# Scores of two attention heads as 64-row products on the two row halves of the TensorE array

## The chip, the cores and the metric

The kernel runs on one core of a Trainium2 chip. The metric is device time in microseconds (us) for one execution. A profile is one further execution, taken by the hardware profiler; its engines are PE (TensorE matmul), PEld (TensorE weight load), DVE (VectorE), ACT (ScalarE), POOL (GpSimd) and SP (SyncE, which issues all loads and stores here).

## What is computed

A forgetting attention over 8 batches, 8 heads, 576 positions and 64 dimensions per head, and after it a channel mix on the 8 x 64 = 512 joined dimensions. All inputs are float32 or wider; shapes and the parts that matter:

```python
scores = scale * np.matmul(q, k.transpose(0, 1, 3, 2))
causal = np.triu(np.ones((S, S), dtype=bool), k=1)
cum = np.cumsum(np.maximum(s, 0.0), axis=-1)
bias = -(cum[:, :, :, None] - cum[:, :, None, :])
scores = np.where(causal, -1000000000.0, scores + np.minimum(bias, 0.0))
scores = scores - np.max(scores, axis=-1, keepdims=True)
attn = np.exp(scores)
attn = attn / (np.sum(attn, axis=-1, keepdims=True) + 1e-09)
x = np.matmul(attn, v)        # heads joined to 512 columns

xk = mu_k * x + (1.0 - mu_k) * x_prev      # x_prev: x one position earlier
xr = mu_r * x + (1.0 - mu_r) * x_prev
k = np.maximum(xk @ w_k, 0.0)              # 512 -> 1024
out = 1.0 / (1.0 + np.exp(-(xr @ w_r))) * (k * k @ w_v)
```

## The kernel before

**Precision.** Matmuls run on the type float32r, a rounded float32. To keep more bits, an operand is split into a high part (a rounded copy, made by ACT) and a low part (what is left, a subtraction on POOL or DVE), and a product is the sum of several matmuls over such parts in one bank of PSUM.

**Planner.** Nothing is issued in the order of the code. Each operation is added to a `Plan` (lines 54 to 282) with its engine, an estimate of its time, the buffers it reads and writes and a due time. `run` lays out all operations with a list scheduler, forward and backward eight times, keeps the order with the shortest estimate and then emits each engine's instructions in that order. A buffer of a tag with n copies waits for the user n turns before it. Due times only rank what is ready; they hold nothing back.

**Visits.** A visit is one pair of heads of one batch. Batch 0 is visited in two passes, first the tiles 0 to 2 of the queries (`A`), then tiles 3 and 4 (`Z`), four pairs each; the seven later batches have 28 visits with all five tiles (`ALL`). Query tile t covers 64 rows for t = 0 and 128 otherwise, and 64, 192, 320, 448 or 576 keys: the keys up to its last row. Each visit loads Q and K (line 588), K's and Q's parts are made (lines 603 to 618), V is loaded and split (552 to 563), and then, for each head: scores, exponents, normalization, transposes of the attention weights on PE (line 770), their split (797, 801 and others), and the product with V (line 903) into `xT`, which goes to DRAM. Each 256 positions that are complete make one chunk of the channel mix: 18 chunks, matmuls at lines 1040 (w_k), 1082 (w_r) and 1107 (w_v). They fill PE between the attention's steps, and they alone are left after the last visit.

**Q and K.** `load_turned` (573) loads each head's Q and K with their 64 dimensions twice, into partitions 0 to 63 and again into 64 to 127 of one tile: four transfers for Q and four for K per visit. `split_qk` (595) makes for each head `KH`, the rounded K on both halves, and `KL`, the rest on both halves; and `G`, whose lower half is rounded Q and whose upper half is the rest of Q (a cast of 128 partitions on ACT, a subtraction of 64 on POOL). So a 128-row product of G with KH gives (high Q + low Q) times high K, and one with KL the same times low K.

**Scores.** `scores` (625) handles one head. It loads the prefix sums of the gate into `cb`, broadcast over the partitions (line 630); POOL makes from it the causal `mask` (649). `products` (661) takes one bank of the two of tag `s`, puts two matmuls into it (line 678), G with KH and G with KL, and has DVE read it (line 693): a fused add of the bias, scale and running minimum that writes the tile `W` and the negated maximum `nm`. A tile of 576 keys is done in two pieces of 288, so a head with all tiles has six pieces: 64, 192, 320, 448, 288 and 288 keys. Where a piece holds the diagonal block, DVE reads it in two instructions. Then ACT takes the exponent (711) and POOL multiplies by the reciprocal sum (724).

**Buffers.** `cb`, `mask` and `s` have two copies, `raw` four, `G`, `KH` and `KL` three. The score tiles `W` exist in two sets, used by the heads in turn; in the passes `A`, which need only the small tiles, two further sets lie inside the largest tile of each (`early`, 376 to 382).

**Order of a visit.** Line 1248: for each of the two heads in turn, its scores are added, then the weighted sum of the head before (`finish`, 1222); the next visit's preparation comes after the first head's scores. Loads are added one visit ahead (1242 to 1244).

Of the kernel before, what the change touches and what calls it, by code (L numbers as in the profile page):

```python
# [12 lines left out]
F32R = mybir.dt.float32r  # L13
# [272 lines left out]
def forgetting_attention_then_channel_mix(  # L286
# [64 lines left out]
    def dma(emit, reads, writes, ns):  # L351
# [21 lines left out]
        for u in range(2)  # L373
    ]

    early = [w[:3] for w in weights]
    for w in weights:
        early.append([])
        for t in range(3):
            c = sum(KN[:t])  # L380
            early[-1].append(fixed(w[NQ - 1].ap[:, c : c + KN[t]]))
        w[NQ - 1].last = early[-1]

    for w in early:
        nc.gpsimd.memset(w[0].ap[64:P], 0.0)
# [187 lines left out]
    def load_turned(src, b, hp, a, e, tag, plain):  # L573

        if plain:
            x = sbuf([P, e - a], tag, 3)
            dma(
                lambda: nc.sync.dma_start(
                    x.get(), src[b, 2 * hp : 2 * hp + 2, :, a:e].rearrange("h d t -> (h d) t")
                ),  # L580
                [], [(x, 0), (x, 1)], 819 * (e - a) / S,
            )
            return [x]
        xs = [sbuf([P, e - a], "raw", 4) for _ in range(2)]
        for j in range(2):
            for r in range(2):
                dma(
                    lambda j=j, r=r: nc.sync.dma_start(
                        xs[j].get()[64 * r : 64 * r + 64], src[b, 2 * hp + j, :, a:e]
                    ),  # L590
                    [], [(xs[j], r)], 410 * (e - a) / S,
                )
        return xs

    def split_qk(qs, ks):

        nq, nk = qs[0].n, ks[0].n
        G = [sbuf([P, nq], "G", 3, F32R) for _ in range(2)]
        KH, KL = ([sbuf([P, nk], x, 3, F32R) for _ in range(2)] for x in ("KH", "KL"))
        for j in range(2):  # L600
            k, kh, kl = ks[j], KH[j], KL[j]
            act(
                lambda k=k, kh=kh: nc.scalar.copy(kh.get(), k.get()),  # L603
                [(k, 0), (k, 1)], [(kh, 0), (kh, 1)], nk, 150,
            )
            pool(
                lambda k=k, kh=kh, kl=kl: nc.gpsimd.tensor_tensor(  # L607
                    out=kl.get(), in0=k.get(), in1=f32(kh.get()), op=ALU.subtract
                ),
                [(k, 0), (k, 1), (kh, 0), (kh, 1)], [(kl, 0), (kl, 1)], nk, 114, 2.21,  # L610
            )
            q, g = qs[j], G[j]
            act(
                lambda q=q, g=g: nc.scalar.copy(g.get(), q.get()),
                [(q, 0), (q, 1)], [(g, 0), (g, 1)], nq, 150,
            )
            pool(
                lambda q=q, g=g: nc.gpsimd.tensor_tensor(  # L618
                    out=g.get()[64:P], in0=q.get()[64:P], in1=f32(g.get()[64:P]), op=ALU.subtract
                ),  # L620
                [(q, 1)], [(g, 1)], nq, 114, 2.21,
            )
        return G, KH, KL

    def scores(b, h, tiles, G, KH, KL):

        NK = KN[tiles[-1]]
        CB = sbuf([P, NK], "cb", 2) if not first else first.pop(0)
        (b == 0 and h < 2 and tiles == A) or dma(
            lambda: nc.sync.dma_start(  # L630
                CB.get(), cum_d.ap[b * H + h : b * H + h + 1, 0:NK].broadcast_to([P, NK])
            ),
            [cum_d], [CB], 819 * NK / S,
        )
        nm, sums, rinv = (sbuf([P, n], x, 2) for x, n in (("nm", 3 * NQ), ("sums", NQ), ("rinv", NQ)))
        if 0 in tiles:
            pool(lambda: nc.gpsimd.memset(sums.get()[:, 0:1], 1.0), [], [(sums, 0)], 1, 36)
        pt = early[h % 4] if tiles == A else weights[h % 2]


        M = sbuf([P, S], "mask", 2)

        def mask(m, k0, n):
# [16 lines left out]

        def products(t, m, i, k0, w, W):
            ps = bank(1, "s", 2)
            q0 = QS[t] - QS[tiles[0]]
            if KL is None:
                r = slice(64 * (h % 2), 64 * (h % 2) + 64)
                pe(
                    lambda: nc.tensor.matmul(
                        ps.get()[:m, :w],
                        G.get()[r, q0 : q0 + m],
                        KH.get()[r, k0 : k0 + w],  # L670
                        start=True,
                        stop=True,
                    ),
                    [(G, x) for x in range(2)] + [(KH, x) for x in range(2)], [ps], w, m, 4 / 2.4, 64,
                )
            for x, K in enumerate((KH, KL) if KL is not None else ()):
                pe(
                    lambda x=x, K=K: nc.tensor.matmul(  # L678
                        ps.get()[:m, :w],
                        G.get()[:, q0 : q0 + m],  # L680
                        K.get()[:, k0 : k0 + w],
                        start=x == 0,
                        stop=x == 1,
                    ),
                    [(G, x) for x in range(2)] + [(K, x) for x in range(2)], [ps], w, m,
                )

            for a, e in ((k0, min(k0 + w, QS[t])), (max(k0, QS[t]), k0 + w)):
                if a >= e:
                    continue  # L690
                bias = CB if a < QS[t] else M
                dve(
                    lambda a=a, e=e, bias=bias, i=i: nc.vector.tensor_tensor_reduce(  # L693
                        out=W.ap[:m, a:e],
                        in0=ps.get()[:m, a - k0 : e - k0],
                        in1=bias.get()[:m, a:e],
                        scale=-SCALE,
                        scalar=3.0e38 if i == 0 else nm.get()[:m, 3 * t + i - 1 : 3 * t + i],
                        op0=ALU.add,
                        op1=ALU.min,  # L700
                        accum_out=nm.get()[:m, 3 * t + i : 3 * t + i + 1],
                    ),
                    [ps, (bias, 0 if bias is CB else t > 0)] + ([(nm, (t, i - 1))] if i else []),
                    [(W, i), (nm, (t, i))], e - a,
                )
                i += 1
            return i

        def exponents(t, m, n, mi, W):
# [12 lines left out]
        def normalize(t, m, n, W):  # L722
# [15 lines left out]
        if 0 in tiles:  # L738
            mask(64, 0, 1)
        mask(P, QS[max(1, tiles[0])], len([t for t in tiles if t]))  # L740
        for t in tiles:
            m, n, W = QN[t], KN[t], pt[t]
            i = 0
            for k0, w in [(0, n)] if n <= 512 else [(0, n // 2), (n // 2, n // 2)]:
                i = products(t, m, i, k0, w, W)
            exponents(t, m, n, i - 1, W)
        pool(
            lambda: nc.gpsimd.tensor_scalar(
                out=rs(rinv), in0=rs(sums), scalar1=1.0e-9, scalar2=None, op0=ALU.add
            ),  # L750
            [(sums, t) for t in tiles], [rinv], len(tiles), 100,
        )
        dve(lambda: nc.vector.reciprocal(rs(rinv), rs(rinv)), [], [rinv], 8 * len(tiles))  # L753
        for t in tiles:
            normalize(t, QN[t], KN[t], pt[t])
        return pt
# [435 lines left out]
    def load(n):  # L1192
        b, hp, tiles = visits[n]
        q0, q1 = QS[tiles[0]], QS[tiles[-1]] + QN[tiles[-1]]
        loaded[n] = (
            load_turned(q, b, hp, q0, q1, "G", n < PLAINQ),
            load_turned(k, b, hp, 0, q1, "KH", n < PLAINQ),
        )

    def prepare(n):  # L1200
# [3 lines left out]
        QKs[n] = (qs * 2, ks * 2, [None] * 2) if n < PLAINQ else split_qk(qs, ks)  # L1204
        Vs[n] = vn if n < PLAIN else split_v(vn, vn.n // P)
# [12 lines left out]
    pend = None  # L1218
# [20 lines left out]
    for n, (b, hp, tiles) in enumerate(visits):  # L1239
# [8 lines left out]
        for j in range(2):  # L1248
            plan.due = due + j * step
            pt = scores(b, 2 * hp + j, tiles, *(x[j] for x in QKs[n]))  # L1250
            if pend is not None:
                finish(*pend)
            pend = (j, pt, Vs[n], xT, n, due + (j + WDUE) * step)
# [53 lines left out]
```

## Time and profile before

| | |
|---|---|
| runs shown | 919.32, 919.80, 922.17 us; median 919.8 |
| profiled execution | span 919.5 us, beside which the profile gives no other time; its mean granted TensorE clock 0.965 |
| instructions | 18649 |
| moved by DMA | 110.89 MB; HBM read 90.64 MB, written 19.04 MB |
| loads of Q and K | 240 of 144 KB, 32 of 80 KB, 16 of 64 KB |
| prefix sums (`cb`) | 64 loads of 288 KB, 6 of 160 KB |
| transposes (line 770) | 960 matmuls |
| scores (line 678) | 768 matmuls |

How to read its views. The page gives each engine's busy time, its share of the span and its count of instructions, and the clock that the throttle granted to TensorE in 40 slices of the span (tenths of full speed). The view by stretches gives the same busy times for any part of the span, or for one line of the code. The groups of instructions give line, engine, operation, the names of the tiles written and read, the shape and the count. The timeline lists instructions by their start. Matmuls are pipelined, so the recorded length of one overlaps the start of the next, and the ends are modelled; a PE that is busy all the time may still wait a little in it. A wait is put down to the instruction that released it.

### The profile page before, as it was taken

What the parts mean: (1) busy time and instruction counts of PE and PEld (TensorE: products, weight loads), DVE (VectorE), ACT (ScalarE), POOL (GpSimd) and SP (SyncE); (2) the same over time, 40 slices, a digit from 0 to 9 for tenths busy, and PEclk for the clock granted to TensorE, in tenths of its full rate; (3) what the DMA queues carried; (4) which work ended last, traced back from release to release, by engine and by line L of the source; (5) the groups of instructions that cost most, each with busy time, mean ns of one, the idle gap of its engine ahead of it and who ended that gap; (6) DMA issues with size and microseconds to landing.
All of it is one profiled execution on the core that took longest, in us unless ns stands there. A gap on an engine that the chain in (4) does not pass through costs nothing. (4 is left out here: it accounts for less than half of the span.)

```text
span 919.5 us, 18649 instructions
## 1 busy us (share of the span) xinstructions
PE 872.8 (95%) x5546; PEld 758.6 (83%) x5546; DVE 696.3 (76%) x2473; ACT 693.1 (75%) x1834; POOL 519.1 (56%) x884
## 2 busy tenths in 40 slices
PE   6877879999999999999999999999999999998998
PEld 4656858987988898988889898989898979887886
DVE  6897998987987788778878778777787887546431
ACT  5888888998997898788968787878787876445331
POOL 6999599898576566556665646565556461100000
PEclk7568989999999999999999999999999999999999
DMA  6798645645344343434353525252434230101100
GB/s 195 223 257 237 206 123 160 174 142 168 100 151 129 109 152 87 145 112 144 100 151 93 163 61 159 79 152 79 147 97 138 79 89 25 42 31 35 46 24 23
DMA packets 65045, 110.89 MB, mean 121 GB/s; under 512 B 10544, under 2 KB 26416, under 8 KB 64944
## 3 DMA queue, kind: packets, MB, share of 16 engines
q1 hardware_dynamic: 64944, 109.71, 40.2%
q8 instruction: 43, 0.70, 0.3%
q14 instruction: 58, 0.48, 0.2%
HBM read 90.64 MB, written 19.04 MB: 119 GB/s over the span
## 5 line engine op out<-in xcount | busy, mean ns | idle before, releaser
L1040 PE MATMUL m<-xh,w_k 128*128 128x256 f32 x1152 | 231.4, 287 | 4.4 <-DVE kl L1069 4.4
L711 ACT ACTIVATE W<-W,nm 64x64 f32<-64x64 f32 (+4 forms) x320 | 179.7, 562 | 41.3 <-DVE nm L693 36.7
L770 PE MATMUL t<-ident,W 128*128 128x128 f32 (+1 forms) x960 | 188.3, 284 | 16.6 <-DVE ph L844 4.8
L1107 PE MATMUL m<-w_v,kh 128*128 128x512 f32 x576 | 198.4, 403 | 0.0
L1040 PEld LDWEIGHTS m<-xh,w_k 128*128 128x128 f32 x1152 | 186.2, 190 | 6.2 <-DVE kl L1069 4.8
L724 POOL TENSOR_SCALAR W<-W,rinv 64x64 f32<-64x64 f32 (+4 forms) x320 | 165.2, 538 | 10.6 <-DVE rinv L753 6.1
L1040 PE MATMUL m<-xl,w_k 128*128 128x256 f32 x576 | 164.6, 286 | 0.0
L770 PEld LDWEIGHTS t<-ident,W 128*128 128x128 f32 (+1 forms) x960 | 114.3, 133 | 47.5 <-DVE pl L801 7.9
L607 POOL TENSOR_TENSOR KL<-raw,KH 128x576 fp32r<-128x576 f32 (+1 forms) x72 | 98.5, 1370 | 79.8 <-ACT KH L603 73.4
L678 PE MATMUL s<-KH,G 128*128 128x288 f32 (+4 forms) x384 | 125.3, 335 | 11.3 <-ACT KH L603 5.3
L801 DVE TENSOR_TENSOR pl<-t,ph 128x256 fp32r<-128x256 f32 (+3 forms) x264 | 122.2, 472 | 16.0 <-ACT ph L797 14.7
L1107 PEld LDWEIGHTS m<-w_v,kh 128*128 128x128 f32 x576 | 106.2, 189 | 18.2 <-DVE r L530 0.2
L678 PE MATMUL s<-KL,G 128*128 128x288 f32 (+4 forms) x384 | 118.5, 312 | 2.4 <-POOL KL L607 2.4
L797 ACT CAST ph<-t 128x256 fp32r<-128x256 f32 (+3 forms) x264 | 107.3, 414 | 13.0 <-PE t L770 11.5
L1107 PE MATMUL m<-w_v,kl 128*128 128x512 f32 x288 | 117.0, 406 | 0.0
L693 DVE CUSTOM_DVE_ANT_0 W<-s,cb 128x320 f32<-128x320 f32 (+3 forms) x256 | 94.9, 375 | 26.4 <-PE s L678 21.7
L903 PE MATMUL po<-ph,V 128*128 128x448 f32 (+4 forms) x344 | 109.6, 326 | 3.7 <-ACT ph L797 1.8
L1040 PEld LDWEIGHTS m<-xl,w_k 128*128 128x128 f32 x576 | 109.2, 190 | 0.9
L618 POOL TENSOR_TENSOR G<-raw,G 64x576 fp32r<-64x576 f32 (+2 forms) x72 | 93.6, 1300 | 27.4 <-issue 13.2
L988 DVE SCALAR_TENSOR_TENSOR xp<-x,mu,xp 128x256 f32<-128x256 f32 (+3 forms) x192 | 80.4, 419 | 37.2 <-ACT xp L979 33.9
L979 ACT ACTIVATE xp<-x,mu 128x256 f32<-128x256 f32 (+3 forms) x192 | 81.5, 424 | 29.3 <-DVE xl L1011 9.7
L1082 PE MATMUL m<-w_r,xh 128*128 128x512 f32 x288 | 101.9, 407 | 0.0
(97 smaller groups left out, 1751.7 us busy)
## 6 DMA issues: line engine op xcount, KB each, us to landing
raw<-in_k SPq DMA_DIRECT2D x128, 144.0 KB, 3.2
cb<-cum_d SPq DMA_DIRECT2D x64, 288.0 KB, 3.6
raw<-in_q SPq DMA_DIRECT2D x112, 144.0 KB, 3.3
vn<-in_v SPq DMA_DIRECT2D x32, 320.0 KB, 3.8
out<-g SPq DMA_DIRECT2D x36, 256.0 KB, 2.1
x_d<-xT SPq DMA_DIRECT2D x28, 288.5 KB, 2.3
x<-x_d SPq DMA_DIRECT2D x12, 514.0 KB, 4.0
w_k<-in_moe_w_k SPq DMA_DIRECT2D x8, 512.0 KB, 5.3
```

What stands on the lines that cost most here:

```text
L607: lambda k=k, kh=kh, kl=kl: nc.gpsimd.tensor_tensor(out=kl.get(), in0=k.get(), in1=f32(kh.get()), op=ALU.subtract),
L678: lambda x=x, K=K: nc.tensor.matmul(ps.get()[:m, :w], G.get()[:, q0 : q0 + m], K.get()[:, k0 : k0 + w], start=x == 0, stop=x == 1,),
L693: lambda a=a, e=e, bias=bias, i=i: nc.vector.tensor_tensor_reduce(out=W.ap[:m, a:e], in0=ps.get()[:m, a - k0 : e - k0], in1=bias.get()[:m, ...
L711: lambda: nc.scalar.activation(W.ap[:m, :n], W.ap[:m, :n], AF.Exp, bias=nm.get()[:m, 3 * t + mi : 3 * t + mi + 1], scale=-1.0, accum_out=s ...
L724: lambda: nc.gpsimd.tensor_scalar(out=W.ap[:m, :n], in0=W.ap[:m, :n], scalar1=rinv.get()[:m, t : t + 1], scalar2=1.0, op0=ALU.mult, op1=AL ...
L770: lambda: nc.tensor.transpose(ps.get()[0:m, place : place + P], pt[t].ap[:, k0 : k0 + m], ident.ap),
L797: act(lambda: nc.scalar.copy(strips(ph), src()), [ps], [(ph, k) for k in ks], n * m)
L801: lambda: nc.vector.tensor_tensor(out=strips(pl), in0=src(), in1=f32(strips(ph)), op=ALU.subtract),
L903: lambda: nc.tensor.matmul(po.get()[: P if both else 64, at + q0 - base : at + q0 - base + m], V.get()[:, kb, 2 * j : 2 * j + (2 if both e ...
L1040: lambda u=u, f=f, c=c, n=n, w=w, x=x: nc.tensor.matmul(ps.get()[:, u * CT : (u + 1) * CT], weight["k", c, f // 4].get()[:, w, f % 4 * P : ...
L1082: lambda c=c, n=n, x=x, w=w: nc.tensor.matmul(ps.get(), x.get()[:, c, ts], weight["r", c, 0].get()[:, w], start=c == 0 and n == 0, stop=c ...
L1107: lambda f=f, n=n, x=x, w=w: nc.tensor.matmul(ps.get(), x.get()[:, f, ts], weight["v", f, 0].get()[:, w], start=f == 0 and n == 0, stop=f ...
```

## The change

The two heads of a visit lie side by side: the even head's 64 dimensions on partitions 0 to 63, the odd head's on 64 to 127. `load_pair` loads Q of both with one transfer, and K with another. `split_pair` makes a high and a low part of each tile, `QH` and `QL`, `KH` and `KL`, each for both heads at once, in two copies each. `scores` handles both heads. A piece takes both banks of `s`, one for each head, and puts three matmuls into each: high Q with high K, low Q with high K, high Q with low K (the product of the two low parts, which the kernel before contains, is left out). Each reads 64 partitions, the even head's the lower half and the odd head's the upper; the two heads' matmuls alternate, and the six are emitted as one operation of the planner. The stationary operand always has 128 columns, in the first piece too. DVE then reads the two banks as before.

With it go: four full sets of `W` in place of two with the two inner ones; four copies of the small sums; the weighted sums of the previous visit's two heads are added after this visit's scores of both; the next visit's preparation after those. A constructor's argument sets a smaller scratch space for dynamic DMA. The argument lists of `exponents` and `normalize` change to fit.

```diff
@@ -370,18 +370,9 @@
 
     weights = [
         [fixed(const.tile([P, KN[t]], F32, name=f"W{t}_{u}")) for t in range(NQ)]
-        for u in range(2)
+        for u in range(4)
     ]
-
-    early = [w[:3] for w in weights]
     for w in weights:
-        early.append([])
-        for t in range(3):
-            c = sum(KN[:t])
-            early[-1].append(fixed(w[NQ - 1].ap[:, c : c + KN[t]]))
-        w[NQ - 1].last = early[-1]
-
-    for w in early:
         nc.gpsimd.memset(w[0].ap[64:P], 0.0)
 
 
@@ -570,77 +561,39 @@
-    def load_turned(src, b, hp, a, e, tag, plain):
...
-        xs = [sbuf([P, e - a], "raw", 4) for _ in range(2)]
-        for j in range(2):
-            for r in range(2):
...
-    def split_qk(qs, ks):
...
-    def scores(b, h, tiles, G, KH, KL):
+    def load_pair(src, b, hp, a, e):
+
+        x = sbuf([P, e - a], "raw", 4)
+        dma(
+            lambda: nc.sync.dma_start(
+                x.get(), src[b, 2 * hp : 2 * hp + 2, :, a:e].rearrange("h d t -> (h d) t")
+            ),
+            [], [x], 819 * (e - a) / S,
+        )
+        return x
+
+    def split_pair(x, tag):
+
+        n = x.n
+        hi, lo = (sbuf([P, n], tag + y, 2, F32R) for y in "HL")
+        act(lambda: nc.scalar.copy(hi.get(), x.get()), [x], [hi], n, 150)
+        pool(
+            lambda: nc.gpsimd.tensor_tensor(
+                out=lo.get(), in0=x.get(), in1=f32(hi.get()), op=ALU.subtract
+            ),
+            [x, hi], [lo], n, 114, 2.21,
+        )
+        return hi, lo
+
+    def scores(b, hp, tiles, Q, K):
+        heads = (2 * hp, 2 * hp + 1)
+        QH, QL = Q
+        KH, KL = K
+        CBs, Ms, pts, stats = [], [], [], []
+
+        def mask(CB, M, m, k0, n):
...
@@ -658,55 +611,75 @@
-        def products(t, m, i, k0, w, W):
-            ps = bank(1, "s", 2)
...
-            for x, K in enumerate((KH, KL) if KL is not None else ()):
...
+        for h in heads:
+            CB = sbuf([P, NK], "cb", 2) if not first else first.pop(0)
+            (b == 0 and h < 2 and tiles == A) or dma(
+                lambda CB=CB, h=h: nc.sync.dma_start(
+                    CB.get(), cum_d.ap[b * H + h : b * H + h + 1, 0:NK].broadcast_to([P, NK])
+                ),
+                [cum_d], [CB], 819 * NK / S,
+            )
+            st = [sbuf([P, n], x, 4) for x, n in (("nm", 3 * NQ), ("sums", NQ), ("rinv", NQ))]
+            if 0 in tiles:
+                pool(
+                    lambda x=st[1]: nc.gpsimd.memset(x.get()[:, 0:1], 1.0),
+                    [], [(st[1], 0)], 1, 36,
+                )
+            M = sbuf([P, S], "mask", 2)
+            if 0 in tiles:
+                mask(CB, M, 64, 0, 1)
+            mask(CB, M, P, QS[max(1, tiles[0])], len([t for t in tiles if t]))
+            CBs.append(CB)
+            Ms.append(M)
+            stats.append(st)
+            pts.append(weights[h % 4])
+
+        def products(t, m, i, k0, w):
+            pss = [bank(1, "s", 2) for _ in heads]
+
+            def emit():
+                for n, (G, K) in enumerate(((QH, KH), (QL, KH), (QH, KL))):
+                    for j in range(2):
+                        r = slice(64 * j, 64 * j + 64)
+                        nc.tensor.matmul(
+                            pss[j].get()[:, :w],
+                            G.get()[r, q0 : q0 + P],
+                            K.get()[r, k0 : k0 + w],
+                            start=n == 0,
+                            stop=n == 2,
+                        )
+
+            x = plan.add(
+                "PE", max(3 * w * 1.0625 / 2.4, 330.0), emit, [QH, QL, KH, KL], pss, land=0.83 * P + 1
+            )
+            plan.columns[x] = 3 * w
+
+            for j in range(2):
+                ps, CB, M, (nm, _, _), W = pss[j], CBs[j], Ms[j], stats[j], pts[j][t]
+                y = i
+                for a, e in ((k0, min(k0 + w, QS[t])), (max(k0, QS[t]), k0 + w)):
+                    if a >= e:
+                        continue
+                    bias = CB if a < QS[t] else M
+                    dve(
...
+                        [(W, y), (nm, (t, y))], e - a,
+                    )
+                    y += 1
+            return y
+
+        def exponents(t, m, n, mi, W, nm, sums):
@@ -735,25 +708,28 @@
...
         for t in tiles:
+            m, n = QN[t], KN[t]
             i = 0
             for k0, w in [(0, n)] if n <= 512 else [(0, n // 2), (n // 2, n // 2)]:
+                i = products(t, m, i, k0, w)
+            for j in range(2):
+                exponents(t, m, n, i - 1, pts[j][t], *stats[j][:2])
+        for j in range(2):
...
@@ -1192,17 +1168,14 @@
     def load(n):
         b, hp, tiles = visits[n]
         q0, q1 = QS[tiles[0]], QS[tiles[-1]] + QN[tiles[-1]]
-        loaded[n] = (
-            load_turned(q, b, hp, q0, q1, "G", n < PLAINQ),
-            load_turned(k, b, hp, 0, q1, "KH", n < PLAINQ),
-        )
+        loaded[n] = (load_pair(q, b, hp, q0, q1), load_pair(k, b, hp, 0, q1))
 
     def prepare(n):
         qs, ks = loaded.pop(n)
         b, hp, tiles = visits[n]
         vn = load_values(b, hp, -(-KN[tiles[-1]] // P), n < PLAIN)
-        QKs[n] = (qs * 2, ks * 2, [None] * 2) if n < PLAINQ else split_qk(qs, ks)
-        Vs[n] = vn if n < PLAIN else split_v(vn, vn.n // P)
+        QKs[n] = split_pair(qs, "Q"), split_pair(ks, "K")
+        Vs[n] = split_v(vn, vn.n // P)
 
     plan.due = -3000.0
     loaded = {}
@@ -1245,17 +1218,17 @@
         plan.due = due
         xT = sbuf([P, S + 1], "xT", 2)
         pool(lambda xT=xT: nc.gpsimd.memset(xT.get()[:, 0:1], 0.0), [], [(xT, 2)], 1, 36)
-        for j in range(2):
-            plan.due = due + j * step
-            pt = scores(b, 2 * hp + j, tiles, *(x[j] for x in QKs[n]))
-            if pend is not None:
-                finish(*pend)
-            pend = (j, pt, Vs[n], xT, n, due + (j + WDUE) * step)
-            if j == 0 and n + 1 < len(visits):
-                plan.due = due + SPLIT * step
-                prepare(n + 1)
+        plan.due = due
+        pts = scores(b, hp, tiles, *QKs[n])
+        for x in pend:
+            finish(*x)
+        pend = [(j, pts[j], Vs[n], xT, n, due + (j + WDUE) * step) for j in range(2)]
+        if n + 1 < len(visits):
+            plan.due = due + SPLIT * step
+            prepare(n + 1)
         if n == len(visits) - 1:
-            finish(*pend)
+            for x in pend:
+                finish(*x)
         while done_chunks < NCHUNK:
             end = (done_chunks + 1) * CT - 1
             if end % S >= there[end // S]:
@@ -1276,7 +1249,7 @@
     import concourse.bacc as bacc
     from concourse.bass_utils import run_bass_kernel_spmd
 
-    nc = bacc.Bacc("TRN2", target_bir_lowering=False, num_devices=1)
+    nc = bacc.Bacc("TRN2", target_bir_lowering=False, num_devices=1, dynamic_dma_scratch_size=1024)
     arrays, args = {}, []
     for name in _INS:
         a = inputs[name]
```

More of the change, by code (lines that the diff above doesn't have):

```diff
@@ L595, in split_qk @@
-    def split_qk(qs, ks):
-        nq, nk = qs[0].n, ks[0].n
-        G = [sbuf([P, nq], "G", 3, F32R) for _ in range(2)]
-        KH, KL = ([sbuf([P, nk], x, 3, F32R) for _ in range(2)] for x in ("KH", "KL"))
-        for j in range(2):
[L601 to L623, printed above, removed]
@@ L625, in scores @@
-    def scores(b, h, tiles, G, KH, KL):
-        NK = KN[tiles[-1]]
[L628 to L643, printed above, removed]
+    def load_pair(src, b, hp, a, e):
[7 more added lines that the diff above has]
+        return x
@@ L659, in mask @@
             )
-        def products(t, m, i, k0, w, W):
-            ps = bank(1, "s", 2)
-            q0 = QS[t] - QS[tiles[0]]
[L664 to L675, printed above, removed]
-            for x, K in enumerate((KH, KL) if KL is not None else ()):
[L677 to L707, printed above, removed]
@@ L709, in exponents @@
-        def exponents(t, m, n, mi, W):
+        for h in heads:
[20 more added lines that the diff above has]
+            pts.append(weights[h % 4])
@@ new lines, in products @@
+        def products(t, m, i, k0, w):
+            pss = [bank(1, "s", 2) for _ in heads]
+            q0 = QS[t] - QS[tiles[0]]
+            def emit():
[21 more added lines that the diff above has]
+                    dve(
+                        lambda a=a, e=e, bias=bias, y=y, ps=ps, nm=nm, W=W: nc.vector.tensor_tensor_reduce(
+                            out=W.ap[:m, a:e],
+                            in0=ps.get()[:m, a - k0 : e - k0],
+                            in1=bias.get()[:m, a:e],
+                            scale=-SCALE,
+                            scalar=3.0e38 if y == 0 else nm.get()[:m, 3 * t + y - 1 : 3 * t + y],
+                            op0=ALU.add,
+                            op1=ALU.min,
+                            accum_out=nm.get()[:m, 3 * t + y : 3 * t + y + 1],
+                        ),
+                        [ps, (bias, 0 if bias is CB else t > 0)] + ([(nm, (t, y - 1))] if y else []),
+                        [(W, y), (nm, (t, y))], e - a,
+                    )
+                    y += 1
+            return y
@@ L720, in exponents, with normalize @@
             )
-        def normalize(t, m, n, W):
+        def normalize(t, m, n, W, rinv):
             pool(
@@ L736, in rs @@
             return x.get()[:, tiles[0] : tiles[-1] + 1]
-        if 0 in tiles:
-            mask(64, 0, 1)
-        mask(P, QS[max(1, tiles[0])], len([t for t in tiles if t]))
         for t in tiles:
-            m, n, W = QN[t], KN[t], pt[t]
+            m, n = QN[t], KN[t]
             i = 0
             for k0, w in [(0, n)] if n <= 512 else [(0, n // 2), (n // 2, n // 2)]:
[L745 to L756, printed above, removed]
+                i = products(t, m, i, k0, w)
+            for j in range(2):
+                exponents(t, m, n, i - 1, pts[j][t], *stats[j][:2])
+        for j in range(2):
+            _, sums, rinv = stats[j]
+            pool(
+                lambda sums=sums, rinv=rinv: nc.gpsimd.tensor_scalar(
+                    out=rs(rinv), in0=rs(sums), scalar1=1.0e-9, scalar2=None, op0=ALU.add
+                ),
+                [(sums, t) for t in tiles], [rinv], len(tiles), 100,
+            )
+            dve(
+                lambda rinv=rinv: nc.vector.reciprocal(rs(rinv), rs(rinv)),
+                [], [rinv], 8 * len(tiles),
+            )
+            for t in tiles:
+                normalize(t, QN[t], KN[t], pts[j][t], rinv)
+        return pts
     def weighted(j, pt, V, xT, tiles, plain):
@@ L1217, in forgetting_attention_then_channel_mix @@
         load_weight("r", c, 0, moe_w_r, R0 + RS * c, c)
-    pend = None
+    pend = []
     done_chunks = 0
@@ L1247, in forgetting_attention_then_channel_mix @@
         pool(lambda xT=xT: nc.gpsimd.memset(xT.get()[:, 0:1], 0.0), [], [(xT, 2)], 1, 36)
-        for j in range(2):
-            plan.due = due + j * step
-            pt = scores(b, 2 * hp + j, tiles, *(x[j] for x in QKs[n]))
-            if pend is not None:
-                finish(*pend)
-            pend = (j, pt, Vs[n], xT, n, due + (j + WDUE) * step)
-            if j == 0 and n + 1 < len(visits):
-                plan.due = due + SPLIT * step
-                prepare(n + 1)
+        plan.due = due
[6 more added lines that the diff above has]
+            prepare(n + 1)
         if n == len(visits) - 1:
-            finish(*pend)
+            for x in pend:
+                finish(*x)
         while done_chunks < NCHUNK:
```

16 lines of the change are left out of this document (removed).

## The prediction

> **What bounds the kernel now.** The page first: its span, the engines' busy shares, and the row of the granted TensorE clock in 40 slices.
>
> ```profile
> span 919.5 us, 18649 instructions
> PE 872.8 (95%) x5546; PEld 758.6 (83%) x5546; DVE 696.3 (76%) x2473; ACT 693.1 (75%) x1834; POOL 519.1 (56%) x884
> PEclk7568989999999999999999999999999999999999
> ```
>
> The profiled execution spans 919.5 us and the median of the runs shown is 919.8, so a sum made against the span needs no correction. PE is busy 95%, but an average over stages decides nothing, so next comes the busy time in three stretches (columns: length, busy time and instructions of PE, PEld, DVE, ACT and POOL, clock, DMA share, GB/s).
>
> ```profile
> 0.00:140.00 140.00, 108.02 (x556) 83.75 (x556) 120.66 (x408) 111.23 (x294) 117.13 (x205) 0.77 0.70 204
> 140.00:780.00 640.00, 631.86 (x4216) 560.08 (x4216) 514.19 (x1947) 527.86 (x1431) 399.15 (x674) 1.00 0.41 121
> 780.00:920.00 140.00, 132.88 (x777) 114.79 (x775) 61.44 (x120) 54.05 (x111) 2.80 (x6) 1.00 0.10 34
> ```
>
> From 140 to 780 us PE idles 8 of 640 us at a clock of 1.00: this stretch is as long as PE's instruction stream. The first 140 us are a ramp with four engines loaded (DVE 121, POOL 117, ACT 111 us) and PE idle for 32 us at a clock of 0.77. The last 140 us hold no scores. The list of waits agrees: what a score's load waits for its bank's reader is 13 us in all.
>
> ```profile
> PEld s L678 <- DVE nm L693: 13.0, 28, 1.2
> ```
>
> So a step off PE is worth time in the ramp at most, and a step on PE is worth its whole length in the 640 us, as far as the others keep up.
>
> **The change on PE.** A matmul's recorded length is modelled and overlaps the next, so I price by distance from start to start. The timeline (start, length, what):
>
> ```profile
> 501.48 0.19 PE L678 MATMUL s<-KH,G 128*64 128x64 f32 x1
> 501.51 0.22 PE L678 MATMUL s<-KL,G 128*64 128x64 f32 x1
> 501.57 0.34 PE L678 MATMUL s<-KH,G 128*128 128x192 f32 x1
> ...
> 502.84 0.31 PE L678 MATMUL s<-KH,G 128*128 128x320 f32 x1
> 502.98 0.31 PE L678 MATMUL s<-KL,G 128*128 128x320 f32 x1
> 503.13 0.27 PE L770 MATMUL t<-ident,W 128*128 128x128 f32 x1
> ...
> 504.14 0.37 PE L678 MATMUL s<-KH,G 128*128 128x448 f32 x1
> 504.35 0.36 PE L678 MATMUL s<-KL,G 128*128 128x448 f32 x1
> 504.55 0.36 PE L903 MATMUL po<-pl,V 128*64 128x448 f32 x1
> 504.75 0.31 PE L903 MATMUL po<-ph,V 128*128 128x320 f32 x1
> 504.90 0.31 PE L903 MATMUL po<-pl,V 128*64 128x320 f32 x1
> ...
> 506.65 0.29 PE L678 MATMUL s<-KH,G 128*128 128x288 f32 x1
> 506.79 0.29 PE L678 MATMUL s<-KL,G 128*128 128x288 f32 x1
> 506.92 0.39 PE L1107 MATMUL m<-w_v,kh 128*128 128x512 f32 x1
> ```
>
> Two of 448 columns take 0.41 us (0.205 each), two of 320 take 0.29 (0.145), two of 288 take 0.27 (0.135), two of 64 take 0.09 (0.045). The weight loads:
>
> ```profile
> 501.54 0.19 PEld L678 LDWEIGHTS s<-KH,G 128*128 128x128 f32 x1
> 501.65 0.19 PEld L903 LDWEIGHTS po<-ph,V 128*128 128x128 f32 x1
> ```
>
> A load of 128 columns is followed by the next after 0.11 us. So a product of 192 columns (0.145 x 192/320 = 0.087 us of streaming) is held by its load: 0.11. Now a head has two matmuls for each of the pieces 64, 192, 320, 448, 288 and 288. Per pair of heads: 4x0.045 + 4x0.11 + 4x0.145 + 4x0.205 + 8x0.135 = 3.10 us.
>
> After it each piece is six matmuls of 64 rows for both heads, in three rounds of two. That two of them on opposite row halves run at one time appears in no row. From below, a round costs one matmul of its width; from above, two. I take the lower end: nothing the two use is common (partitions 0 to 63 and 64 to 127 of the same tiles, two banks), and the rows show the array streaming one product while the load for another is under way, so parts of it do work at one time. For the loads of a round the bounds are one load (0.11) and two (0.22), taken at one for the same reason; this is the weaker choice, since every pair of loads above has a distance between its starts. The load of the first piece now has 128 columns. Per pair: 3x0.11 + 3x0.11 + 3x0.145 + 3x0.205 + 6x0.135 = 2.52 us, that is 0.58 less.
>
> How many pairs count? The matmuls of the score line, in the whole and in the saturated stretch:
>
> ```profile
> L678 PE MATMUL s<-KH,G 128*128 128x288 f32 x128 | 43.4, 341 | 2.9 <-DVE nm L693 2.7
> 140.00:780.00 640.00, 141.07 (x644) 100.12 (x644) 1.00 0.41 121
> ```
>
> 128 of the 288 form are four per pair, so 32 pairs; 644 matmuls at 24 a pair are 26.8 pairs in the stretch. PE there shrinks by 26.8 x 0.58 = **15.6 us**.
>
> A change between 128-row and 64-row matmuls occurs twice per piece, at most 12 x 26.8 = 322 times in the stretch. No row shows one. The nearest is the change of column count above: 128*128 to 128*64 and back at 448 and 320 columns, starts 0.20, 0.20, 0.15 apart, which is bare streaming. That gives nothing. From above, a change that let nothing overlap would cost what successive matmuls now overlap: 0.29 - 0.135 = 0.155 us. I take nothing. The Trainium skill (TensorEngine Tiling (Array Packing), Key Properties) says that changing the tiling mode, not just the tile, drains TensorE; no run here shows a change of row mode, and what a drain would make is the third rival. The Trainium skill (TensorE: Matmul & The Clock Gate, Part 3) has packed matmuls start about 4 ns apart; by that figure the 18 rounds of a pair would cost 2 us more over the stretch, an estimate, and no row shows it yet.
>
> **The change off PE.** Splits on ACT and POOL, whole program (the rows of KL and of G on POOL), and loads:
>
> ```profile
> 0.00:920.00 920.00, 98.50 (x72) 0.96 0.41 121
> 0.00:920.00 920.00, 93.58 (x72) 0.96 0.41 121
> raw<-in_k SPq DMA_DIRECT2D x128, 144.0 KB, 3.2
> raw<-in_q SPq DMA_DIRECT2D x112, 144.0 KB, 3.3
> ```
>
> Each pair keeps half: POOL loses about 96 of its 519 us, and ACT two of its four casts a pair. A full pair's eight loads of 144 KB become two of 288 KB: half the bytes, six issues fewer on SP, none moved behind another queue. None of it is on the path of the saturated stretch (POOL 399 and ACT 528 of 640 us), so there I count nothing. It may tell in the ramp:
>
> ```profile
> 20.00:100.00 80.00, 63.97 (x316) 49.42 (x315) 69.97 (x238) 64.55 (x181) 69.99 (x121) 0.69 0.82 240
> 0.00:100.00 100.00, 17.26 (x16) 0.71 0.80 231
> 0.00:100.00 100.00, 12.87 (x15) 0.71 0.80 231
> ```
>
> POOL is busy 70 of the 80 us from 20 to 100, and the last two rows (KL and G within 100 us) give 30 us, of which 15 go. DVE is nearly as full (70 of 80) and loses nothing, so the next bound is close: at most 12 us of the ramp (DVE's idle 10 and some of the start), and below nothing if the joined heads hold it up: they tie both score banks and both cb tiles to one visit. I put the loss at 4 us at worst and take a gain of **5 us**, nearest to DVE's bound, in which the ramp's few scores on PE are contained.
>
> Costed at nothing: four sets of W and of the small sums in place of two, which only remove waits (the memsets of W stay four); the constructor's smaller scratch, since the loads listed are issued by SP's queue; finishing a visit's two heads together, since PE has channel mix to fill the gap, and without it would stall as in the fourth rival.
>
> Sum: 919.5 - 15.6 - 5 = 898.9, **899 us**.
>
> **An added wait.** A piece now fills both score banks, and the next piece starts only when DVE has read both. Queued behind a waiting matmul on PE is all of channel mix. DVE's score work and the mask's and cb's rows:
>
> ```profile
> 0.00:920.00 920.00, 218.02 (x1280) 0.96 0.41 121
> 0.00:920.00 920.00, 54.53 (x136) 0.96 0.41 121
> cb<-cum_d SPq DMA_DIRECT2D x64, 288.0 KB, 3.6
> 502.50 0.25 PE L678 MATMUL s<-KL,G 128*128 128x192 f32 x1
> 503.01 0.21 DVE L693 CUSTOM_DVE_ANT_0 W<-s,cb 128x64 f32<-128x64 f32 x1
> ```
>
> Per pair DVE takes 218/32 = 6.8 us, PE 2.5, the next masks 54.5/32 = 1.7, the next cb 3.6, and twelve hand-offs of 0.26 (502.75 to 503.01) 3.1: 17.7 us. The pace is 640/26.8 = 23.9 us a pair, so 6 us are left and I count no stall.
>
> **The rivals.** Of the forecast's 20.6 us each keeps what it does not touch.
>
> 1. *Loads of a round don't overlap* (the slower side). Place: each piece's six loads; price 6 x 0.11 = 0.66 us a piece, 3.96 a pair, 0.86 above now, x 26.8 = 23.0, less 5: **937.5 us**. For: the loads quoted come one by one. Against: they all used the same rows. It decides for slower from (3.10 + 5/26.8)/36 = 0.091 us a load.
> 2. *Nothing overlaps; the change doesn't do what it says*: every piece six matmuls in a row, 5.04 a pair, 52.0 more, less 5: **966.5 us**. Against: as above, separate partitions and banks.
> 3. *A change of row mode stalls the array*: 322 x 0.155 = 49.9, less 20.6: **949 us**, at half that price 924; even at 0.064 us each. Against: the column changes cost nothing.
> 4. *The joined hand-offs take over*: DVE has other work for 80% of the stretch and each hand-off queues behind it; 0.5 us more on each of twelve uses up the 6 us. The stretch then keeps its old pace and the ramp its length: **about 920 us**.
>
> **How the numbers follow.** Forecast 0.63, its own range 886 (ramp 12, and 21 in place of 15.6 if idle PE goes too) to 912 (ramp 4 lost, hand-offs 8 of stall). Rivals: loads 0.09, no overlap 0.08, mode 0.13, hand-offs 0.07. This kernel's measurement tells about 0.3% (2.8 us) from no change. Faster takes the forecast (0.61), a third of the mode rival and half of the last: 0.68; same 0.06; slower 0.26 from the first two and the rest. The range goes from 886 to 945: it leaves out 966 (0.08), a full stall at 949 (0.07) and 0.04 below.
>
> **What would show it.** The two matmuls of a round starting well under 0.1 us apart, and a piece of 288 over in 0.40 us (0.66 by rival 1, 0.81 by rival 2); the first matmul after a piece starting as usual (rival 3: some 0.15 late); PE idle of 8 us in the stretch staying under 16 (rival 4); POOL's busy time near 423 us. Wrong would be any piece longer than now.

## The result and the profile after

The change makes the kernel slower: 949.15 us median against 919.56 of the kernel before in the same series, a ratio of 1.0315 (taken over all runs, not from the two medians; 95% interval 1.0296 to 1.0333). That is 29.6 us more where about 20 us less was forecast, and above the end of the range at 945.

First the page of the changed kernel: span, busy shares, granted clock, memory traffic, and the splits on POOL.

```profile
span 947.7 us, 18612 instructions
...
PE 913.9 (96%) x5955; PEld 746.7 (79%) x5955; DVE 696.4 (73%) x2473; ACT 660.8 (70%) x1762; POOL 421.0 (44%) x812
...
PEclk7668979999999999999999999999999999999999
...
HBM read 71.11 MB, written 19.04 MB: 95 GB/s over the span
...
L581 POOL TENSOR_TENSOR QL<-raw,QH 128x576 fp32r<-128x576 f32 (+2 forms) x36 | 47.4, 1318 | 267.2 <-ACT QH L579 267.0
```

The work off PE shrank as planned: POOL lost 98 us, ACT 32, HBM reads fell from 90.6 to 71.1 MB. PE grew from 873 to 914 us of busy time, and it is still the bound, as the stretches show (columns as before):

```profile
0.00:140.00 140.00, 116.69 (x679) 86.20 (x679) 122.33 (x442) 108.36 (x297) 105.28 (x203) 0.77 0.59 190
140.00:780.00 640.00, 636.27 (x4307) 521.51 (x4306) 493.45 (x1851) 482.02 (x1312) 306.03 (x590) 1.00 0.29 93
```

PE idles under 4 of the 640 us from 140 to 780, less than the 8 before, and the clock there is 1.00. So no wait took over; PE's own stream became longer. Where it became longer is seen in the timeline of one piece of 288 keys in the midst of channel mix, first PE and then the weight loads (start, length, what, how many in the merged row):

```profile
500.39 0.28 PE L1016 MATMUL m<-xl,w_k 128*128 128x256 f32 x1
500.50 0.28 PE L1016 MATMUL m<-xh,w_k 128*128 128x256 f32 x1
500.71 0.40 PE L645 MATMUL s<-KH,QH 64*128 64x288 f32 x2
500.95 0.29 PE L645 MATMUL s<-KH,QL 64*128 64x288 f32 x2
501.08 0.29 PE L645 MATMUL s<-KL,QH 64*128 64x288 f32 x2
501.30 0.39 PE L1016 MATMUL m<-xh,w_k 128*128 128x256 f32 x1
501.53 0.28 PE L1016 MATMUL m<-xl,w_k 128*128 128x256 f32 x1
501.65 0.28 PE L1016 MATMUL m<-xh,w_k 128*128 128x256 f32 x1
```

```profile
500.39 0.19 PEld L1016 LDWEIGHTS m<-xh,w_k 128*128 128x128 f32 x1
500.71 0.19 PEld L645 LDWEIGHTS s<-KH,QH 64*128 64x128 f32 x2
500.82 0.19 PEld L645 LDWEIGHTS s<-KH,QL 64*128 64x128 f32 x2
500.95 0.18 PEld L645 LDWEIGHTS s<-KL,QH 64*128 64x128 f32 x2
501.30 0.19 PEld L1016 LDWEIGHTS m<-xh,w_k 128*128 128x128 f32 x1 [0.16 <-issue]
501.41 0.19 PEld L1016 LDWEIGHTS m<-xl,w_k 128*128 128x128 f32 x1
```

Four things are to be read here. First, the two matmuls of a round do run at one time: both of the second round lie within 0.29 us, the length that a single matmul of 288 columns had before; over all rounds of this trace the second of the two starts 3 ns after the first in the median. Second, so do their two loads, both within 0.19 us, the length of one. Third, the second and third rounds start 0.13 us apart, bare streaming. Fourth, the edges are new. Before the first round the start is 0.21 us after the last matmul of channel mix, where matmuls of that form follow each other after 0.11 to 0.12; and its load starts at that same moment, while in the stream a load starts one matmul earlier (500.39 for the matmul of 500.50). After the last round the same: the next load starts at 501.30 with 0.16 us in which no load was under way, and the matmul behind it is followed after 0.23 in place of 0.12. From 500.50 to 501.53 there are 1.03 us for work of 0.12 + 3 x 0.135 + 0.12 = 0.645: **0.385 us lost on a piece**, at the two changes of row mode. From its first round to the next matmul (500.71 to 501.30) the piece takes 0.59 us for both heads, where the four matmuls of the kernel before take 4 x 0.135 = 0.54.

### The profile page after: what moved, and what is told of

It is laid out like the page before. It is cut to its first block, busy times and chain, and to the rows that moved or that the text cites. A ratio compares the mean times of both kernels' runs of the same rounds, so it can differ in the third digit from the quotient of the medians.

```text
span 947.7 us, 18612 instructions
## 1 busy us (share of the span) xinstructions
PE 913.9 (96%) x5955; PEld 746.7 (79%) x5955; DVE 696.4 (73%) x2473; ACT 660.8 (70%) x1762; POOL 421.0 (44%) x812
## 4 chain that ended last, share of the span: by engine, by line
PE 79%; DVE 8%; ACT 7%; issue 2%; POOL 2%; DMA 1%; SPq 0%; POOLq 0%; DVEq 0%; ACTq 0%
PE m L1016 21%; PE m L1083 19%; PE s L645 10%; PE t L746 10%; PE m L1058 10%; PE po L879 8%; ACT xp L955 2%; DVE xp L964 2%; ACT W L684 2%; DVE W L666 1%; PE t L879 1%; ACT xh L983 1%; POOL W L697 1%; DVE xl L987 1%; DVE pl L777 1%
## 5 line engine op out<-in xcount | busy, mean ns | idle before, releaser
L1016 PE MATMUL m<-xh,w_k 128*128 128x256 f32 x1152 | 239.9, 292 | 2.4 <-DVE kl L1045 2.3
L1083 PE MATMUL m<-w_v,kh 128*128 128x512 f32 x576 | 203.6, 412 | 1.3 <-DVE r L521 1.3
L746 PE MATMUL t<-ident,W 128*128 128x128 f32 (+1 forms) x960 | 192.9, 287 | 10.6 <-DVE pl L812 4.1
L1016 PE MATMUL m<-xl,w_k 128*128 128x256 f32 x576 | 167.2, 290 | 0.4 <-DVE xl L987 0.4
L581 POOL TENSOR_TENSOR QL<-raw,QH 128x576 fp32r<-128x576 f32 (+2 forms) x36 | 47.4, 1318 | 267.2 <-ACT QH L579 267.0
L879 PE MATMUL po<-ph,V 128*128 128x448 f32 (+4 forms) x344 | 112.6, 333 | 4.0 <-DVE xT L913 1.9
L964 DVE SCALAR_TENSOR_TENSOR xp<-x,mu,xp 128x256 f32<-128x256 f32 (+3 forms) x192 | 80.4, 419 | 41.8 <-ACT xp L955 39.1
L666 DVE CUSTOM_DVE_ANT_0 W<-s,cb 128x192 f32<-128x192 f32 (+3 forms) x256 | 87.9, 376 | 24.9 <-PE s L645 22.1
L879 PE MATMUL po<-pl,V 128*64 128x448 f32 (+4 forms) x280 | 93.8, 346 | 1.3 <-DVE pl L777 1.1
L645 PE MATMUL s<-KH,QH 64*128 64x288 f32 (+4 forms) x384 | 81.2, 408 | 7.6 <-ACT KH L579 4.7
L879 PEld LDWEIGHTS po<-ph,V 128*128 128x128 f32 x344 | 68.6, 200 | 17.0 <-ACT ph L773 6.2
```

What stands on the lines that cost most here:

```text
L645: nc.tensor.matmul(pss[j].get()[:, :w], G.get()[r, q0 : q0 + P], K.get()[r, k0 : k0 + w], start=n == 0, stop=n == 2,)
L746: lambda: nc.tensor.transpose(ps.get()[0:m, place : place + P], pt[t].ap[:, k0 : k0 + m], ident.ap),
L879: lambda: nc.tensor.matmul(po.get()[: P if both else 64, at + q0 - base : at + q0 - base + m], V.get()[:, kb, 2 * j : 2 * j + (2 if both e ...
L964: lambda n=n, o=o, i=i, to=to: nc.vector.scalar_tensor_tensor(out=to(), in0=x.get()[:, c, o + i : o + i + n], scalar=mu1.ap[:, which, c : ...
L1016: lambda u=u, f=f, c=c, n=n, w=w, x=x: nc.tensor.matmul(ps.get()[:, u * CT : (u + 1) * CT], weight["k", c, f // 4].get()[:, w, f % 4 * P : ...
L1083: lambda f=f, n=n, x=x, w=w: nc.tensor.matmul(ps.get(), x.get()[:, f, ts], weight["v", f, 0].get()[:, w], start=f == 0 and n == 0, stop=f ...
```

## The experiments

Theory A holds the changes between 128-row and 64-row matmuls responsible. Rival B was the joined hand-offs: both banks of a piece must be read before the next piece starts. Later rivals are named in the expectations. The kernel before was at 920.3, 920.4 and 921.2 us in the three series.

**Fewer changes of mode.** Pieces that fit into one bank together are issued as one group:

```diff
-            for k0, w in [(0, n)] if n <= 512 else [(0, n // 2), (n // 2, n // 2)]:
-                i = products(t, m, i, k0, w)
...
+            groups = [[(2, 0, 320, 0), (1, 0, 192, 320)], [(3, 0, 448, 0), (0, 0, 64, 448)]] + groups
...
+        for group in groups:
+            pss = products(group)
```

> The changed kernel with its 64-row products in fewer groups: the pieces of 64 and 448 keys share one bank of each head and are issued as one group of twelve matmuls, and so do 192 and 320; four groups a pair in place of six (132 in all in place of 192), the same matmuls, columns and reads. Theory A (the stall at a change between 128-row and 64-row matmuls): in the changed kernel's trace a group takes some 0.39 us more than its three rounds (the matmul before it is followed 0.09 later than usual, the group is 0.19 over its rounds, the matmul after it is followed 0.11 late). 60 groups fewer, 56 of them where PE is the bound: 949 - 22 = 927 us. Theory B (the joined hand-offs hold PE up: both banks of a piece have to be read before the next): fewer and longer groups, whose reads on DVE come in longer bursts, give no gain: 949 or a little above.

Measured: 932.0 us, ratio 1.0131 (1.0114 to 1.0149), 17 us below the changed kernel. That is A's direction and three quarters of its amount; B expected none. This kernel also has another order of the planner; what that can be worth is seen further down.

**No change of mode.**

```diff
-                for n, (G, K) in enumerate(((QH, KH), (QL, KH), (QH, KL))):
+                for n, (G, K) in enumerate(((QH, KH), (QL, KL))):
                     for j in range(2):
-                        r = slice(64 * j, 64 * j + 64)
+                        r = slice(0, P)
...
-                "PE", max(3 * w * 1.0625 / 2.4, 330.0), emit, [QH, QL, KH, KL], pss, land=0.83 * P + 1
...
+                "PE", max(4 * w * 1.0625 / 2.4, 440.0), emit, [QH, QL, KH, KL], pss, land=0.83 * P + 1
```

> The changed kernel with its score products on all 128 rows, two matmuls for each head and piece in place of three on 64 rows: no change of row mode remains, everything else of the change stays (one load and one split for both heads, joined banks, four sets of W). The scores of both heads become a sum over both heads' dimensions, so the output is another. Theory A: PE pays 4 x 0.11 + 4 x 0.11 + 4 x 0.145 + 4 x 0.205 + 8 x 0.135 = 3.36 us a pair, against 3.60 for the groups of the changed kernel plus 6 x 0.20 outside them, 4.80: 32 x 1.44 = 46 us less, 903 us. Theory B: the hand-offs stay as they are, so the time stays above 940 us.

Measured: 923.62 us, ratio 1.0040 (1.0027 to 1.0053). B, above 940, falls: the hand-offs are the same as in the changed kernel. But it is 25.5 us below the changed kernel, not 46. Two reasons for the gap were still open here: pieces in the ramp, where PE isn't the bound, had been counted; and the planner had been given other estimates and made another order.

**More changes of mode, with a control.** One matmul more in the two pieces of 288 keys, after the first round or after the last:

```diff
+                    if w == 288 and n == 0:
+                        nc.tensor.matmul(
+                            pss[0].get()[:, :64], none.ap, KH.get()[:, k0 : k0 + 64],
+                            start=False, stop=False,
+                        )
```

> The changed kernel with one more matmul of 128 rows and 64 columns, with a stationary operand of zeros, between the first and second round of the two pieces of 288 keys: it adds nothing to the scores, costs some 0.11 us by itself and adds two changes of row mode in 64 groups. Theory A: 64 x (0.39 + 0.11) = 32 us more, a few less where PE isn't the bound: about 977 us. Theory B: only its own length: 64 x 0.11 = 7 us more, 956 us.

> The control of the run before: the same additional matmul of 128 rows after the third round of the two pieces of 288 keys, where the row mode changes anyway. Theory A: no additional change, and the load that stands open after a group is now that of the additional matmul: between 2 and 7 us more than the changed kernel, 951 to 956 us. Theory B: the same 956 us as for the run before.

Measured: 976.77 us (ratio 1.0631, 1.0604 to 1.0659) and 954.87 us (1.0385, 1.0365 to 1.0405). Both kernels hold the same instructions, planned from the same estimates, and differ only in where the 128-row matmul stands. Their traces show one order, that of the changed kernel. 64 more pairs of changes cost 21.9 us: **0.342 us for a pair of changes**, 0.171 each if the two are alike. B said 956 for both.

The traces, both at a clock of 1.00 here, agree. From the first round of a piece to the second matmul behind it pass 1.25 us in the first (309.40 to 310.65, in the first of the two timelines further down) and 0.93 in the control, 0.32 us less:

```profile
301.52 0.40 PE L647 MATMUL s<-KH,QH 64*128 64x288 f32 x2
...
302.12 0.30 PE L655 MATMUL s<-KH,none 128*128 128x64 f32 x1
302.25 0.36 PE L1023 MATMUL m<-xl,w_k 128*128 128x256 f32 x1
302.45 0.39 PE L1023 MATMUL m<-xh,w_k 128*128 128x256 f32 x2
```

The control isn't free of open loads either: its 256 columns at 302.25 are followed after 0.20 us, where 0.12 is usual, since the added matmul is too short to cover the next load. With these 0.08 us a pair of changes costs 0.40, beside 0.385 read on the piece of the changed kernel. So the price lies between 0.32 and 0.40 us. Two things blur the average over whole runs: some ten of the 64 pieces lie in the first 140 us, where PE isn't the bound, and the mean clock of the runs was 0.956 against the control's 0.961, by estimate (0.006 of 975 us) up to 6 of the 21.9 us.

**What the stall consists of.** The first of these again, with a stationary operand of 32 columns:

> The run split_group (977 us) with 32 columns of zeros in place of 128 in the stationary operand of the additional matmul, in the same order. Its load is shorter by about 0.08 us (0.11 x 96/128). If the stall at a change of mode is a drain with the next load left open behind it, the shorter load shows in full: 64 x 0.08 = 5 us less, 972 us. If it is a drain alone with loads hidden: 977 us.

Measured: 971.88 us (ratio 1.0562, 1.0544 to 1.0580), 4.9 us less. The timelines agree, first with 128 columns (with what follows the piece), then with 32:

```profile
309.40 0.40 PE L647 MATMUL s<-KH,QH 64*128 64x288 f32 x2
309.73 0.30 PE L655 MATMUL s<-KH,none 128*128 128x64 f32 x1
309.96 0.40 PE L647 MATMUL s<-KH,QL 64*128 64x288 f32 x2
310.20 0.29 PE L647 MATMUL s<-KL,QH 64*128 64x288 f32 x2
310.42 0.39 PE L1023 MATMUL m<-xl,w_k 128*128 128x256 f32 x1
310.65 0.40 PE L1023 MATMUL m<-xh,w_k 128*128 128x256 f32 x2
```

```profile
308.29 0.40 PE L647 MATMUL s<-KH,QH 64*128 64x288 f32 x2
308.62 0.22 PE L655 MATMUL s<-KH,none 128*32 128x64 f32 x1
308.77 0.40 PE L647 MATMUL s<-KH,QL 64*128 64x288 f32 x2
```

The added matmul takes 0.23 us of PE with a load of 128 columns and 0.15 with one of 32: the load stands in the path in full. At a change of mode the next load isn't prepared under the running matmul, as it is in the stream of channel mix (the load of 500.39 for the matmul of 500.50), and some 0.1 us (0.21 against 0.11 to 0.12 at the entry) pass before it starts.

**The same order.** To take the planner out of the comparison, two full-row matmuls again, with the estimates of the changed kernel left in place:

> The changed kernel with two matmuls on all 128 rows for each head and piece in place of three on 64 (the scores become a sum over both heads' dimensions), but with the planner's estimates left as they are, so that the order is that of the changed kernel. Theory A: about 157 of the 192 groups lie where PE is the bound and stall by 0.34 us each (the difference of split_group and group_end, 21.9 us over 64), 53 us; the products on 128 rows cost 26.8 x 0.84 = 22 us more: 949 - 53 + 22 = 918 us. Theory B: above 940 us.

Measured: 920.59 us, ratio 0.9997 (0.9986 to 1.0007), near A's 918 and far from B's 940. In the traces DVE, ACT and POOL run the same instructions in the same order as in the changed kernel. In one order, then, 64-row products cost 949.15 - 920.59 = 28.6 us more than full-row ones (the two are from different series, whose kernels before differ by 1.7 us, and whose mean clocks are 0.964 and 0.968, by estimate up to 4 us). Of the 192 groups, those after the ramp can be counted in the changed kernel by the score line's stretch:

```profile
140.00:948.00 808.00, 105.94 (x942) 69.02 (x942) 0.99 0.25 80
```

942 matmuls are 157 groups or 26.2 pairs. With the 0.84 us a pair that the full-row products take longer, (28.6 + 26.2 x 0.84) / 157 = 0.322 us a group, beside the 0.342. This is a net price: by the two pages PE idles 917.9 - 876.1 = 41.8 us in this run and 947.7 - 913.9 = 33.8 in the changed kernel, so the stalls also fill 8.0 us in which PE would have waited anyway. With them it is 58.6 / 157 = 0.373 us, beside the 0.385 of the piece.

**The rest of the change, and a version that might beat both.** If only the stalls are bad, the new layout should be kept where PE isn't the bound:

```diff
+    PAIRED = 8
...
+        QKs[n] = (
+            (split_pair(qs, "Q"), split_pair(ks, "K")) if n < PAIRED else split_qk(qs, ks)
+        )
```

> The new layout (one load, one split, 64-row products for both heads) for the eight visits of batch 0 alone, where PE is not the bound, and the old one (two loads and splits, 128-row products, head by head) for the 28 visits after it; four sets of W throughout. Theory A (the stalls at changes of row mode cost time only where PE is the bound; the rest of the change is worth 3 to 5 us in the ramp: the full-row run paid 26.8 x 0.26 = 7 us more for its products in the saturated stretch and came out 3.4 above before): 915 to 917 us beside 920. Rival C (that gain is not of the ramp, but of the waits that shorter splits and more sets of W spare PE later): 919 to 921 us.

Measured: 929.09 us, ratio 1.0102 (1.0085 to 1.0118): slower than before, outside both expectations. Its companions in the same series each put one part of the change, or of what it saves, into the kernel before:

> The kernel before with four sets of W and of the small sums, its only change (loads, splits and products as before). Theory A: nothing waited long for a W buffer where PE is the bound: 919 to 921 us. Rival C: two to four us less, 916 to 918.

> The kernel before with Q and K of the even head loaded alone, and used for both heads (the odd head's Q and K are left out); the splits stay two. Half the bytes of Q and K. If the loads hold up the ramp: about 916 us. If POOL's splits do: no change, 919 to 921.

> The kernel before with all its loads, but with the even head's parts of Q and K made alone, and used for both heads (the odd head's are left out). POOL loses some 96 us and ACT some 45 in all, as with the change. If POOL's splits hold up the ramp: about 915 us. If the loads do: no change, 919 to 921.

Measured: 926.26 us (1.0066, 1.0048 to 1.0083), 924.54 (1.0045, 1.0032 to 1.0058) and 932.59 (1.0121, 1.0104 to 1.0139). All three take work or waits away, and all are slower. (The run with four sets has the change's smaller scratch space as well, and the mixed layout a still smaller one, which their expectations don't say.) None of the expectations had that. What they share is a new plan: a change of an estimate or a dependence can make the list scheduler lay out the whole kernel anew. So two runs that change nothing but a nanosecond in an estimate:

```diff
-    def act(emit, reads, writes, n, extra=51, table=0):
+    def act(emit, reads, writes, n, extra=52, table=0):
```

> The kernel before, with one constant of the planner's estimates moved by one: 52 in place of 51 ns beside the columns of an operation on ACT. The same operations, in another order of the planner. Theory D (each new plan costs some time against the order of before, whatever else is changed: the four runs made from before's parts lost 4 to 12 us with no or less work): 923 to 932 us. Theory E (the order is worth less than 2 us, and those four lost by what they changed): 918 to 922 us.

> As the run before, with 69 in place of 68 ns beside the columns of an operation on DVE. Theory D: 923 to 932 us. Theory E: 918 to 922 us.

Measured: 934.06 us (1.0142, 1.0112 to 1.0172) and 923.69 (1.0040, 1.0023 to 1.0057). The same operations in another order take 2.5 and 12.8 us more. That is theory D's side: a new order alone is worth up to 13 us here, as much as the spread of the four runs above it (4.2 to 12.2). It can account for all four; that it does so in each isn't shown. In the worse one the stretch that was saturated shows it (columns as before):

```profile
140.00:780.00 640.00, 626.71 (x4134) 551.41 (x4133) 508.00 (x1914) 519.95 (x1407) 397.74 (x672) 0.99 0.42 120
```

PE idles 13 us there, against 8 in the order of before, its clock is 0.99 in place of 1.00 (by estimate, from 0.01 of 640 us, up to 6 us), and it gets 82 fewer matmuls done. So what the halved loads and splits are worth by themselves can't be told from these runs, nor whether the mixed layout would gain in a luckier order; that stays open.

## Why the prediction was wrong

**What bounds the kernel** was right: PE's stream sets the time from 140 us on, in both kernels.

**The rounds** were right in both choices made without a row: the two halves run at one time, and so do their loads. Rivals 1 and 2 fall with it, by the timeline after. The matmuls of a round start 3 ns apart in the median, close to the 4 ns that the prediction set beside its sum. Yet the forecast's sign, a piece of 288 keys over in 0.40 us, did not come: it takes 0.59, since the first round waits for its load and the first matmul behind the piece is held up.

**The step that failed** is the one on the change of row mode: "That gives nothing. ... I take nothing." It was bounded between 0 and 0.155 us a change, and the lower end was taken from the nearest row, the change of column count, which costs nothing. The runs show 0.171 us a change (0.342 for a pair), and the trace of a piece 0.385 for the pair, 0.19 each: over the upper end. The upper end left out that the next load would stand open. The row that was nearest in form was of another kind. There the load of the operand with 64 columns starts at 501.25, a whole matmul ahead of its own at 501.48:

```profile
501.25 0.14 PEld L678 LDWEIGHTS s<-KH,G 128*64 128x64 f32 x1
```

With another count of rows the load is not prepared ahead: at 500.71 load and matmul start together. The Trainium skill (TensorEngine Tiling (Array Packing), Key Properties) says that a change of tiling mode drains TensorE. The trace of the changed kernel agrees for a change of rows, with 0.1 us before the first load; the open load of 0.11 us behind it comes on top.

**Rival 3**, given 0.13, was what happened. It was priced at 322 x 0.155 = 49.9 us and 949; with the 157 groups after the ramp and the 0.385 of the piece it is 157 x 0.385 = 60.4. Against it stand 26.2 x 0.58 = 15.2 us saved in the rounds, which leaves 45.2 us more where 29.6 were measured. The full-row run in the same order tells where the difference went: 8.0 us are waits that the stalls filled, and that run is 0.6 us faster than before although its products cost 26.2 x 0.26 = 6.8 us more on PE, so layout and order together are worth some 7 us. The two weren't separated. That the rival's 949 was met to a fraction of a microsecond is therefore largely luck: its price per change was too low, and what it left out made up for that.

**The gain off PE** (5 us): not settled. The 7 us just named fit a gain of that size, and in the ramp of that run PE idles 28 us where it idled 32 before (one profile each):

```profile
0.00:140.00 140.00, 112.31 (x621) 91.90 (x622) 124.09 (x449) 110.22 (x299) 105.41 (x204) 0.82 0.58 190
```

But the new order, and a clock of 0.82 in place of 0.77 there, lie within the same numbers.

**The added wait** was right to be costed at nothing: PE's idle time fell. Rival 4 falls. Its working had two misreadings. The 80% of the stretch that DVE is busy with other work contains its own reads of the scores, 182.6 us (line 693, 140 to 780 us); without them it is (514.2 - 182.6) / 640 = 52%. And in the hand-off of 0.26 us DVE was at an earlier instruction until about 503.0 (line 1011, from 502.44, 0.65 us long), so that this isn't the length of a free hand-off.

**A term that was missing** altogether is the plan itself. The prediction summed operations at fixed neighbours; in a kernel whose order is laid out by a scheduler, an edit can also draw a new order, and six runs with one (the four with parts of the change and the two with a nanosecond) are 2.5 to 12.8 us slower.

**Two sums** do not come out as stated, without effect on the outcome. The upper end of the forecast's own range, 912, is with the 4 us lost in the ramp and the 8 us of stall 919.5 - 15.6 + 4 + 8 = 915.9. And the span is not the time: each later run is about 2 us longer than the span of its core, so the forecast is in time nearer 901 than 899.

## What to carry to other kernels

Products on the two row halves of the array did overlap in full here, loads included, but each passage between 128-row and 64-row matmuls cost 0.17 to 0.19 us. By that a group has to save 0.34 to 0.39 us to break even, and here a piece saved 0.58/6 = 0.1. Use them where many rounds stand together, and plan them as one block with its entry and exit in the price. When an order is drawn by a scheduler, run a null edit that only re-plans before a few microseconds are put down to a cause, and compare variants under the same order.

## What the runs showed of the hardware

A change in the number of rows keeps the next weight load from being prepared under the running matmul, in both directions (load and matmul start together at 500.71 and at 501.30), and adds some 0.1 us before that load starts (0.21 us in place of 0.11 to 0.12). A change in the number of columns of the stationary operand, 128 to 64 and back, does neither: 448, 448 and 320 columns start 0.20, 0.20 and 0.15 us apart in the prediction's rows, which is bare streaming. Two loads of 64 rows and 128 columns on the two halves take the time of one (both within 0.19 us).
